# From which block on GpSimd's conversions for a block are split behind the last sum of x: block 6 or block 4

## Chip, core and metric

The kernel runs on one core of a Trainium2 chip. The metric is the device time of one execution in microseconds. Before the change three runs took 195.11, 195.18 and 197.03 us; the median, 195.18 us, is the time to be compared. One execution more was recorded by the hardware profiler; all views of the profile are of that one.

## What is computed

A linear recurrence over the sequence (retention, 4 batches, 8 heads, 768 steps, head dimension 64), whose output is the input of a two-layer block with the Mish activation (width 512, inner width 2048):

```python
for t in range(S):
    state = gamma[None, :, None, None] * state + np.einsum('bhd,bhe->bhde', k[:, :, t], v[:, :, t])
    y[:, :, t] = scale * np.einsum('bhd,bhde->bhe', q[:, :, t], state)
...
x = np.ascontiguousarray(attn_out.transpose(0, 2, 1, 3)).reshape(B * S, H * D)
h = x @ w_in
sp = np.where(h > 20.0, h, np.log1p(np.exp(np.minimum(h, 20.0))))
g = h * np.tanh(sp)
return (g @ w_out).astype(np.float32)
```

## The kernel before

**Chunks and blocks.** The sequence of each batch is cut into chunks of 128 rows, 6 a batch, 24 in all. Chunks are numbered 0 to 23. Block 0 holds chunks 0 to 3, and each of blocks 1 to 10 holds two: block 4 holds chunks 10 and 11, block 6 holds 14 and 15, block 7 holds 16 and 17. As a batch has 6 chunks, the work repeats every three blocks: blocks 4 and 7 do the same on TensorE, and so do blocks 5 and 8.

**One block, from block 4 on.** `mixed_in` (L844) makes h = x·w_in, partly by plain products (L875) and partly by a seven-product scheme for 2x2 halves (L855), which needs four sums of x, and adds its partial results on VectorE (L890); ScalarE applies Mish (L866). `seven` (L927) makes g·w_out by seven products (L949); ScalarE copies partial results (`snap`, L955), and VectorE adds them into the output tile `osb` (`done`, L964 and L962). Within `seven` lies the recurrence of later blocks: `retain` (L585) finishes the scores of the next block, and `ready` (L496) begins the block behind that, from the transposed q and k (`qkt`) and from v. So `seven` of block 4 needs the q, k and v of chunks 14 and 15.

**The sums of x.** `x_sums` (L838) makes the four sums, as fp16 differences in SBUF, on VectorE, one instruction each (L842). Two stand behind the fourth output addition of the block before, two at its end. They are the last thing that VectorE does in `seven`; behind them come the state (L513 to L528) and the mask (L548) of the block to come, and then the additions L890, for which TensorE waits.

**What GpSimd does.** It converts q, k and v of each chunk from fp32 to scaled fp16: q at L422, k at L425 (`casts_qk`), v at L432 (`casts_v`), one instruction each. `cast_behind(blk, i)` (L1274), called in `seven`, first copies one element of a sum of g (L1277), so that GpSimd starts behind that sum, and then converts the two chunks of block blk + 3: both q and k, then both v. Where blk + 1 >= `BACK` it converts only the q and k of the first chunk there. The rest is left to `second_of` (L1246), which the main loop calls ahead of the next block's `mixed_in`: it copies one element of the last sum of x (L1249), and then converts q and k of the second chunk and both v.

**SyncE's queue.** Every load (L162), every transpose of q and k by DMA (L437, `turn_by_dma`) and every store (L234, L1232) is issued by SyncE, in program order. Eight semaphores are used in turn, so a DMA is not issued until the one eight before it has landed. In `next_two` (L1234) both chunks are transposed and then two more are loaded; in `next_one` (L1241) one chunk is loaded and the first chunk is transposed, and the second transpose, the stores and another load follow in `second_of`. `osb` has 5 buffers (two a block), q has 4 load buffers, k and v 6 each.

**What the constants decide.** `ONE`, `MIX` and `BACK` are 3, 4 and 6. The main loop (L1317 to L1347) uses `BACK` in three places: whether `second_of(blk - 1)` is called ahead of block blk (blk >= BACK), whether `seven` of block blk calls `next_one` or `next_two` (blk + 1 >= BACK), and which branch `cast_behind` takes (blk + 1 >= BACK).

Of the kernel before, what the change touches and what calls it, by code (L numbers as in the profile page):

```python
# [16 lines left out]
def kernel(  # L17
# [101 lines left out]
    loaded, cast, qkts, ats, ams, states, mids, us, ys = {}, {}, {}, {}, {}, {}, {}, {}, {}  # L119
    xts, gts, wins, wouts, wtmps = {}, {}, {}, {}, {}  # L120
    gtiles, tmats, gsums = {}, [], []
    ONE, MIX, BACK = 3, 4, 6
    nload, ncast = [0], [0]
    stores, weight_left, wsums = [], [], []

# [1253 lines left out]
```

## Time and profile before

| | |
|---|---|
| median of three runs | 195.18 us |
| the profiled execution: its own time | 197.2 us |
| its span, from the first to the last instruction | 195.4 us |
| TensorE busy | 189.2 us, 97% |
| VectorE busy | 141.5 us, 72% |
| ScalarE busy | 104.1 us, 53% |
| GpSimd busy | 73.8 us, 38% |
| granted TensorE clock | 1.000 |

The profiled execution took 1.8 us more than its span, and 2.0 us more than the median of the runs. Times below are counted from the start of its span. Engines are PE (TensorE matmul), PEld (its weight load), DVE (VectorE), ACT (ScalarE), POOL (GpSimd) and SP (SyncE; SPq its DMA queue). An entry in brackets at the end of a row is the time that the engine sat idle before it, and what released it.

By TensorE's first matmul of `mixed_in` (L855) and of `seven` (first L949 behind it), block 4 runs from 92.78 to 108.33 us, block 5 to 123.27, block 6 to 137.48, block 7 to 151.53 and block 8 to 165.57.

### The profile page before, as it was taken

How to read it: one execution, taken by the hardware profiler on the slowest of the kernel's cores; microseconds unless marked ns; L12 is line 12 of the kernel's file. 1: busy time of each engine (PE TensorE's matmuls, PEld its weight loads, DVE VectorE, ACT ScalarE, POOL GpSimd, SP SyncE). 2: the span in 40 equal slices, each digit the busy share in tenths (PEclk: the TensorE clock that was granted, in tenths of full speed). 3: DMA queues.
4: the chain of work that ended last, by engine and by line, in shares of the span. 5: the costliest groups of instructions: out<-in, count | busy, mean ns of one | idle time of the engine just before them, and what ended most of it. 6: DMA issues, size and time to landing. Idle time of an engine off the chain costs nothing.

```text
span 195.4 us, 7191 instructions
## 1 busy us (share of the span) xinstructions
PE 189.2 (97%) x3124; PEld 161.8 (83%) x3124; DVE 141.5 (72%) x270; ACT 104.1 (53%) x194; POOL 73.8 (38%) x98
## 2 busy tenths in 40 slices
PE   7998999999999999999989999999999999999993
PEld 7756478888888888888968978998998998988993
DVE  0796559886686787987995995965885885875462
ACT  3375766263633633644574574484574664763850
POOL 5362000579209629904807605535625710000000
DMA  5999999999999999999799799979894250300202
GB/s 174 303 311 352 361 386 363 304 305 200 218 233 258 224 243 209 166 269 210 159 235 265 138 244 279 100 189 256 101 251 89 53 152 3 111 0 22 92 29 81
DMA packets 84303, 38.78 MB, mean 198 GB/s; under 512 B 57776, under 2 KB 78896, under 8 KB 84272
## 3 DMA queue, kind: packets, MB, share of 16 engines
q1 hardware_dynamic: 84128, 38.28, 81.8%
q8 instruction: 24, 0.39, 0.9%
q14 instruction: 7, 0.06, 0.1%
q10 hardware_dynamic: 144, 0.05, 0.1%
HBM read 27.31 MB, written 6.29 MB: 172 GB/s over the span
## 4 chain that ended last, share of the span: by engine, by line
PE 87%; DVE 6%; ACT 2%; DMA 2%; issue 1%; POOL 0%; POOLq 0%; DVEq 0%
PE o_ps L949 29%; PE h_ps L646 17%; PE h_ps L875 10%; PE h_ps L855 10%; PE o_ps L703 7%; PE at L451 4%; PE y_ps L559 3%; DMA out_dram<-osb 2%; PE t_ps L255 2%; DVE xt L842 1%; DVE hsum L890 1%; PE u_ps L487 1%; PE at L480 1%; ACT g L866 1%; PE y_ps L381 1%
## 5 line engine op out<-in xcount | busy, mean ns | idle before, releaser
L646 PE MATMUL h_ps<-xt,win 128*128 128x256 f16 (+1 forms) x272 | 34.3, 285 | 0.0
L949 PEld LDWEIGHTS <-gsum 128*128 128x128 f16 x320 | 30.3, 98 | 3.8
L646 PEld LDWEIGHTS <-win 128*128 128x128 f16 x272 | 26.4, 98 | 6.5
L655 ACT ACTIVATE g<-h_ps 128x512 f16<-128x512 f32 x38 | 22.7, 597 | 15.6 <-PE h_ps L646 15.6
L949 PE MATMUL o_ps<-tmat,gsum 128*128 128x256 f16 x240 | 29.8, 273 | 0.0
L875 PE MATMUL h_ps<-xt,win 128*128 128x256 f16 x224 | 29.0, 273 | 0.0
L949 PEld LDWEIGHTS <-g 128*128 128x128 f16 x248 | 23.3, 98 | 3.3 <-ACT g L866 0.6
L964 DVE TENSOR_TENSOR osb<-o_ps,snap 128x256 f32<-128x256 f32 (+1 forms) x33 | 13.7, 417 | 12.9 <-PE o_ps L949 7.6
L955 ACT COPY snap<-o_ps 128x256 f32<-128x256 f32 (+1 forms) x33 | 12.2, 370 | 20.1 <-PE o_ps L949 20.1
L875 PEld LDWEIGHTS <-win 128*128 128x128 f16 x224 | 20.8, 98 | 2.0
L866 ACT ACTIVATE g<-h_ps 128x512 f16<-128x512 f32 x35 | 19.9, 588 | 3.4 <-PE h_ps L875 3.4
L885 ACT COPY hsum<-h_ps 128x512 f32<-128x512 f32 x21 | 12.3, 585 | 14.9 <-PE h_ps L855 14.9
L425 POOL TENSOR_TENSOR qk<-kf,qvs 128x512 f16<-128x512 f32 x18 | 19.0, 1056 | 1.7 <-DMA kf<-in_k_dram 1.7
L422 POOL TENSOR_TENSOR qk<-qf,qvs 128x512 f16<-128x512 f32 x18 | 19.1, 1064 | 1.2 <-DMA qf<-in_q_dram 1.2
L949 PE MATMUL o_ps<-wout,g 128*128 128x256 f16 x160 | 19.4, 273 | 0.1
L432 POOL TENSOR_TENSOR v<-vf,qvs 128x512 f16<-128x512 f32 x18 | 19.1, 1076 | 0.4 <-DMA vf<-in_v_dram 0.3
L1277 POOL COPY summed<-gsum 128x1 f16<-128x1 f16 x7 | 3.0, 422 | 42.9 <-DVE gsum L815 32.1
L890 DVE TENSOR_TENSOR hsum<-h_ps,hsum 128x512 f32<-128x512 f32 x21 | 14.1, 688 | 6.1 <-PE h_ps L855 4.3
L855 PE MATMUL h_ps<-xt,wsum 128*128 128x128 f16 x224 | 15.9, 219 | 0.0
L608 ACT CAST xt<-y_ps 128x512 f16<-128x512 f32 x15 | 10.2, 735 | 10.4 <-PE y_ps L559 10.4
L866 ACT ACTIVATE g<-hsum 128x512 f16<-128x512 f32 x21 | 13.2, 630 | 4.0 <-DVE hsum L890 4.0
L855 PEld LDWEIGHTS <-wsum 128*128 128x128 f16 x224 | 14.0, 98 | 0.4
(112 smaller groups left out, 303.2 us busy)
## 6 DMA issues: line engine op xcount, KB each, us to landing
kf<-in_k_dram SPq DMA_DIRECT2D x24, 256.0 KB, 5.2
vf<-in_v_dram SPq DMA_DIRECT2D x24, 256.0 KB, 5.4
out_dram<-osb SPq DMA_DIRECT2D x22, 256.0 KB, 3.7
qf<-in_q_dram SPq DMA_DIRECT2D x20, 256.0 KB, 5.4
wi<-in_moe_w_in_dram SPq DMA_DIRECT2D x6, 512.0 KB, 8.8
wt<-in_moe_w_out_dram SPq DMA_DIRECT2D x2, 1024.0 KB, 10.3
wt<-in_moe_w_out_dram SPq DMA_DIRECT2D x4, 512.0 KB, 7.6
qfirst<-in_q_dram SPq DMA_DIRECT2D x2, 512.0 KB, 4.6
```

Source lines behind the costliest of these rows:

```text
L422: nc.gpsimd.tensor_tensor(in_place(q16.rearrange("p (w x) d -> p w x d", x=2)), by_head(qf), scale_by_head(qs_two[:, heads]), op=ALU.mult)
L425: nc.gpsimd.tensor_tensor(k16.rearrange("p (y w) d -> p w y d", y=2), kf.rearrange("p (w y) d -> p w y d", y=2), boosts.rearrange("p (w y) ...
L432: nc.gpsimd.tensor_tensor(cast[g][2], loaded.pop(g)[2], vs[g % 2].unsqueeze(2).broadcast_to((P, H, D)), op=ALU.mult)
L646: nc.tensor.matmul(h_ps[:, j, cols], wins[s][f // 2][:, bp, f % 2 * P:(f % 2 + 1) * P], xts[blk][:, bp, cols], start=(bp == 0 and at == 0) ...
L655: nc.scalar.activation(gt, h_ps, AF.Mish, scale=inv_boost3)
L703: nc.tensor.matmul(banks[ij][:, t], x(f)[:, t * P:(t + 1) * P], w(f), start=ij in open_banks, stop=f == fs[-1], skip_group_check=True)
L855: nc.tensor.matmul(o_ps[:, f], w(f // 2, k)[:, f % 2 * P:(f % 2 + 1) * P], x[:, k], start=begin and f == 0 and k == 0, stop=k == 1, skip_g ...
L866: nc.scalar.activation(to, src, AF.Mish, scale=inv_boost3)
L875: nc.tensor.matmul(h_ps[:, f], wins[w][h // 2][:, k, h % 2 * P:(h % 2 + 1) * P], xts[blk][:, k, :2 * C], start=k == 0, stop=k == NBP - 1)
L890: nc.vector.tensor_tensor(m, x, y, op=ALU.add)
L949: nc.tensor.matmul(o_ps[:, cols], x(f), w(f)[:, cols], start=first and z == 0, stop=z == n - 1, skip_group_check=True)
L964: nc.vector.tensor_tensor(dst, o_ps[:, cols], plus, op=ALU.add)
```

## The change

One constant goes from 6 to 4. The program's comparisons with it then hold two blocks sooner:

```diff
-    ONE, MIX, BACK = 3, 4, 6
+    ONE, MIX, BACK = 3, 4, 4
```

The code that it steers:

```python
def second_of(blk):
    g = first[blk] + 6
    if g < NCK:
        nc.gpsimd.tensor_copy(summed, xts[blk + 1][:, 3, TB - 1:])
        casts_qk(g + 1)
        turn_by_dma(g + 1)
        casts_v(g)
        casts_v(g + 1)
    store_due(NFB)
    load_to(g + 4)
...
def next_two(g):
    for n in range(2):
        turn_next(g + n)
    if g == first[ONE] + 6:
        store(2)
    load_to(g + 4)

def next_one(g):
    load_to(g + 3)
    if g < NCK:
        turn_by_dma(g)
...
        elif blk + 1 >= BACK:          # in cast_behind
            cast_to(g - 2)
            casts_qk(g - 2)
            ncast[0] = g
```

In GpSimd's order this moves, for chunks 14 to 17, the second chunk's q and k and both v behind one more one-element copy each (two instructions are added, none is taken out). In SyncE's order it moves these DMAs; their number stays:

- before: transposes of 14 and 15; two stores (block 2's); loads of 16 and 17; two stores (block 3's); transposes of 16 and 17; loads of 18 and 19; two stores (block 4's); load of 20
- after: load of 16; transposes of 14 and 15; four stores (blocks 2's and 3's); loads of 17 and 18; transposes of 16 and 17; two stores (block 4's); loads of 19 and 20

TensorE's, VectorE's and ScalarE's instructions and their order stay as they are.

## The prediction, made before the changed kernel was run

> **What bounds the kernel now.** I read the table of engines first, then the chain of waits, then the stretches block by block, and then the rows of single engines around the two longest blocks.
>
> ```profile
> PE 189.2 (97%) x3124; PEld 161.8 (83%) x3124; DVE 141.5 (72%) x270; ACT 104.1 (53%) x194; POOL 73.8 (38%) x98
> ```
>
> TensorE sets the time: what does not fill one of its gaps is worth nothing. The chain that ended last shows where it has gaps: from 97.03 to 115.03 us it leaves TensorE and runs through VectorE, ScalarE and one store, in blocks 4 and 5 only; in blocks 6 to 9 it is TensorE throughout. So I asked for the busy times by stage, `mixed_in` of blocks 4, 5, 7 and 8 and `seven` of 4 (columns: stretch, its length, busy time and instructions of each engine, granted clock, DMA):
>
> ```profile
> 92.78:100.68 7.90, 7.13 (x90) 6.32 (x88) 7.79 (x14) 4.65 (x9) 4.03 (x4) 1.00 0.85 199
> 100.68:108.33 7.65, 7.62 (x178) 6.49 (x176) 5.03 (x12) 3.78 (x8) 4.29 (x5) 1.00 0.95 231
> 108.33:115.62 7.29, 6.89 (x90) 6.29 (x88) 7.19 (x14) 4.64 (x9) 2.37 (x3) 1.00 0.96 193
> ...
> 137.48:144.17 6.69, 6.69 (x90) 6.25 (x88) 5.62 (x12) 4.94 (x9) 4.19 (x5) 1.00 0.81 139
> ...
> 151.53:158.22 6.69, 6.69 (x91) 6.25 (x89) 5.63 (x12) 4.95 (x9) 4.18 (x5) 1.00 0.49 119
> ```
>
> `mixed_in` takes 7.90 us in block 4 and 7.29 in block 5 (VectorE busy almost all of it), against 6.69 in blocks 7 and 8, which do the same work at the same clock. TensorE's rows name the wait: block 4's last seven-product matmuls (L855) wait for VectorE's addition L890, and VectorE reaches that late because the four sums of x ahead of it are slow. VectorE's time in L842 around the end of blocks 3, 4, 5 and 6:
>
> ```profile
> 100.13 0.61 PE L855 MATMUL h_ps<-xt,win 128*128 128x128 f16 x8 [0.76 <-DVE hsum L890]
> ```
>
> ```profile
> 91.60:95.95 4.35, 3.61 (x4) 1.00 0.70 130
> 107.15:110.90 3.75, 3.00 (x4) 1.00 0.79 130
> 122.10:124.30 2.20, 1.07 (x4) 1.00 1.53 162
> 136.30:138.55 2.25, 1.07 (x4) 1.00 1.69 199
> ```
>
> Four equal instructions: 3.61 and 3.00 us in the first two places, 1.07 in the others. What differs is GpSimd. Its rows at the first place, and VectorE's:
>
> ```profile
> 91.57 1.04 POOL L425 TENSOR_TENSOR qk<-kf,qvs 128x512 f16<-128x512 f32 x1
> 92.57 1.09 POOL L422 TENSOR_TENSOR qk<-qf,qvs 128x512 f16<-128x512 f32 x1
> 93.62 1.09 POOL L425 TENSOR_TENSOR qk<-kf,qvs 128x512 f16<-128x512 f32 x1
> 94.67 2.14 POOL L432 TENSOR_TENSOR v<-vf,qvs 128x512 f16<-128x512 f32 x2
> ```
>
> ```profile
> 91.67 2.13 DVE L842 TENSOR_TENSOR xt<-xt 128x256 f16<-128x256 f16 x2
> 93.73 0.41 DVE L964 TENSOR_TENSOR osb<-o_ps,snap 128x256 f32<-128x256 f32 x1
> 94.06 0.41 DVE L962 COPY osb<-o_ps 128x256 f32<-128x256 f32 x1
> 94.39 1.51 DVE L842 TENSOR_TENSOR xt<-xt 128x256 f16<-128x256 f16 x2
> ```
>
> GpSimd changes instruction at 92.57, 93.62, 94.67 and (half of 2.14 on) 95.7. The first sum ends at 92.75, the second at 93.8, the third at 94.86, the fourth at 95.9: each just behind the next such change, however early it began. The additions between them, which read PSUM, keep their 0.41 us. So a sum of x waits until the GpSimd instruction under way is over. The Trainium skill, "SBUF — State Buffer", section "SBUF: two separate sides", gives a reason: VectorE instructions with two SBUF inputs and GpSimd's share a port pair, an exclusive lock held for the whole instruction. By that rule the trace agrees, with 1.02 to 1.13 us for a sum under GpSimd against the shortest row of 0.279.
>
> **Part 1, conversions moved out of the sums of x.** At the end of block 3, GpSimd's q and k of chunk 14 stay (90.57 to 92.6); chunk 15's q and k and both v, four instructions of 1.04 to 1.09 us, move behind the sums. The first sum still waits for 92.6 and ends at 92.75; the second then takes 0.28 (93.0). The additions L964 and L962 follow at their present spacing of 0.33 (TensorE's operands are there: block 6 does these 1.17 and 1.07 us after its matmul starts, here 92.2 and 93.0), then two sums at 0.27: the end is 94.2 instead of 95.9. VectorE is 1.7 us earlier. From TensorE's start of the block that is 1.42 us, against 1.03 in block 7 (138.51 less 137.48): 0.4 late still. Block 7's second L890 sits idle 0.36 and its third 0.40, waiting for ScalarE and TensorE; that cover takes up the 0.4, so block 4 runs as block 7. It gains 7.90 - 6.69 = 1.21 in `mixed_in`. Its `seven` starts with 16 plain matmuls that need Mish of the late sums: from the first L949 to the 17th is 1.94 us in blocks 4 and 5, and 1.75 in block 7 and 1.74 in block 8; 0.19 goes too. Block 4: 1.40.
>
> At the end of block 4, chunk 16's q and k are done 2.04 us after GpSimd's release (106.55 of the present count), and the sums begin at 107.22: 0.67 later, the same gap as block 5 has now (121.49 and 122.16), where four sums take 1.07. All of it goes: 7.29 - 6.69 = 0.60, and 0.20 in `seven`. Block 5: 0.80.
>
> Sum: 2.20 us. The rest of `seven` is 0.1 us longer in each of blocks 4 and 5 than in 7 and 8 (5.71 and 5.61), spread over the small matmuls of the recurrence; no wait stands beside it. I count 0, with 0.2 as its upper bound.
>
> **Part 2, two one-element copies on GpSimd.** 0.19 us each where they have been seen behind a sum of x (0.52 behind a sum of g). Behind them queue four conversions, 4.1 us, and whoever needs them: in block 4 they run from 94.2 to 98.6. VectorE's next instructions with two SBUF inputs are L528 and the sums of g; in block 7 L528 starts 6.56 us into the block, so here at 99.3, 0.7 clear. `seven` needs the v from its L487 at 104.80, which the gain puts at 103.4. Price: 0; if the cover goes, up to one conversion of 1.04 us per instruction caught.
>
> **Part 3, SyncE's queue.** The load of 16 goes ahead of the transpose of 14, three issues of 0.5 to 1.1 us from 90.14: the transpose, ready at 92.64, slips by 0 to 1 us and is needed at 103.7. The transpose of 15 waits for its k until 96.5, not 94.73; rows of the same step have issues of 1.23 to 2.66 us and landings 3.1 to 5.4 us behind the start: 99.6 to 101.9, needed at 103.7. Behind it queue block 2's two stores, which stand at 96.06 now, then block 3's. They are issued from 97.8 to 98.4 on, and landing takes 1.6 to 4.8 us: the first is out by 103.2 at the latest. `osb` has five buffers, so block 4's second tile reuses block 2's first. It is written by the L964 ahead of the sums of x, now at 106.84, then at 105.4: 2.2 us clear. (The profile puts 1.59 us of idle before that L964 to a store that landed at 106.85. But block 7's same L964 also starts 5.87 us after its first L949, for TensorE; here it is 6.16, of which 0.19 is the slow start. I take the store for a coincidence, worth at most 0.1.) Chunk 17 is loaded behind these stores, from about 100.3; 4.4 to 6.0 us to landing gives 107 for q and k, which GpSimd wants at 108 and 109. The chain of eight semaphores adds at most a wait for the first store in front of 18's loads, which nobody wants before 117. From block 6 on the order is as it is. Price: 0, for those margins.
>
> **The profiled execution and the median.** Taken from the profiled execution: 197.2 - 2.2 = 195.0. Its 2.0 us over the median have no place that I can name; both waits come out of program order and fixed durations, so the whole 2.2 is taken from the median too: 195.18 - 2.20 = 193.0 us. One per cent, 1.95 us or 193.23, is about what a measurement of this kernel can tell from no change.
>
> **Rivals.**
> - The 0.4 us by which block 4's sums stay late does reach TensorE (the third L890 moves by it, or Mish does): gain 1.75, time 193.4. For it: the chunk-14 conversion does overlap the first sum. Against it: the idle entries of 0.36 and 0.40. Chance 0.13.
> - Moved conversions catch later VectorE instructions: if GpSimd starts 0.7 us or more later than I put it, L528 and then the sums of g wait, one conversion each. One or two at 1.04 us in block 4 take half the gain: 194.0, at most 194.3. Against it: block 7 has these rows 1.2 us clear. The page's rule named above says the same of any instruction with two SBUF inputs, and gives no other price. Chance 0.08.
> - It does nothing: the sums are slow for another reason, the DMA traffic or the state of the chip, and stay at 3 us: 195.2. Against it: DMA share is 0.70 and 0.79 there, and 1.53 and 1.69 where they are fast. Chance 0.07.
> - Slower: block 2's stores, now behind the transpose of 15, hold block 4's L964, and with it the sums of x, 1 us for 1 us. It takes from 105.4 on; the gain is eaten at 107.6, and 1% is lost at 109.5, 11 to 12 us after issue, against 4.8 at most in the rows. Four stores and six loads in a row speak for some delay. If one lands at 109.6, the time is 197.2. Chance 0.07.
>
> **How the numbers follow.** The forecast itself has 0.65: a gain of 1.9 to 2.5 us, 192.7 to 193.3. The range takes in the first two rivals and the spread of a median, a few tenths: 192.5 to 194.4. That leaves out the last two rivals, 0.14, and a little of the tails. Faster by over 1%: nearly nine tenths of the forecast's own, 0.57. Slower: 0.07. Within: 0.36.
>
> **What would show it.** In the changed profile: L842 in block 3's end 1.9 to 2.0 us for four (one slow), in block 4's end 1.07; no idle of TensorE before block 4's and 5's last L855; both `mixed_in` at 6.7 us; L964 ahead of the sums waiting for TensorE, not for a store; GpSimd's copy L1249 at about 94.2, and its conversions over before L528. The forecast is wrong if a sum is slow with GpSimd idle, or if a store or a transpose stands as releaser in block 4 or 5.

## The result, and the profile after

| | before | after |
|---|---|---|
| median, 22 runs each | 195.94 us | 194.93 us |
| lowest to highest | 194.87 to 197.22 us | 194.80 to 196.50 us |
| ratio of the times, 95% interval | | 0.9946 [0.9923, 0.9968] |
| profiled execution, its span | 197.2, 195.4 us | 195.02, 193.2 us |

The change gains 1.0 us in the median, half a per cent, and not 2.2. Yet the two profiled executions differ by just the 2.2 that were forecast (195.4 and 193.2). Both are true: the runs before spread over 2.3 us, of which the profiled one was at the upper end, and 18 of the 22 runs after lie between 194.80 and 195.02. The lowest runs of the two kernels are within 0.1 us of each other.

The stretches of the changed kernel, `mixed_in` and `seven` of blocks 4 and 5 in turn (columns: stretch, length, busy time and instructions of PE, PEld, DVE, ACT, POOL, clock, DMA share, GB/s):

```profile
92.77:99.46 6.69, 6.69 (x91) 6.26 (x89) 6.12 (x14) 5.05 (x9) 4.18 (x5) 1.00 1.29 189
99.46:107.00 7.54, 7.54 (x180) 6.68 (x178) 4.89 (x13) 3.57 (x8) 2.51 (x3) 1.00 1.08 290
107.00:113.69 6.69, 6.69 (x91) 6.26 (x89) 5.63 (x12) 4.97 (x9) 4.18 (x5) 1.00 1.15 159
113.69:121.14 7.45, 7.45 (x179) 6.57 (x177) 4.94 (x13) 3.56 (x8) 2.51 (x3) 1.00 1.15 269
```

TensorE is busy through all of them; 7.90, 7.65, 7.29 and 7.65 us have become 6.69, 7.54, 6.69 and 7.45, together 2.12 less. VectorE's and GpSimd's rows at the end of block 3:

```profile
91.66 1.41 DVE L842 TENSOR_TENSOR xt<-xt 128x256 f16<-128x256 f16 x2
92.99 0.42 DVE L964 TENSOR_TENSOR osb<-o_ps,snap 128x256 f32<-128x256 f32 x1
93.32 0.41 DVE L962 COPY osb<-o_ps 128x256 f32<-128x256 f32 x1
93.65 0.48 DVE L842 TENSOR_TENSOR xt<-xt 128x256 f16<-128x256 f16 x2
```

```profile
91.56 1.04 POOL L425 TENSOR_TENSOR qk<-kf,qvs 128x512 f16<-128x512 f32 x1
94.27 0.19 POOL L1249 COPY summed<-xt 128x1 f16<-128x1 f16 x1 [1.67 <-DVE xt L842]
```

Only the first sum still waits, for the conversion of chunk 14's k; the four take 1.89 us instead of 3.61. And the output addition ahead of the sums of block 5, the one that block 2's stores might have held, waits for TensorE:

```profile
105.51 0.42 DVE L964 TENSOR_TENSOR osb<-o_ps,snap 128x256 f32<-128x256 f32 x1 [1.68 <-PE o_ps L949]
```

So the question is not where 1.1 us of the gain went in the changed kernel, but why most executions of the kernel before, in this measurement, did not have 2.2 us to lose.

### The profile page after: what moved, and what is told of

Read it like the earlier page. It is cut to its first block, busy times and chain, and to the rows that moved or that the text cites. A ratio compares the mean times of both kernels' runs of the same rounds, so it can differ in the third digit from the quotient of the medians.

```text
span 193.2 us, 7199 instructions
## 1 busy us (share of the span) xinstructions
PE 188.3 (97%) x3124; PEld 162.2 (84%) x3124; DVE 138.3 (72%) x270; ACT 104.4 (54%) x194; POOL 74.0 (38%) x100
## 4 chain that ended last, share of the span: by engine, by line
PE 96%; ACT 1%; issue 1%; POOL 0%; DVE 0%; POOLq 0%
PE o_ps L949 32%; PE h_ps L646 17%; PE h_ps L875 13%; PE h_ps L855 12%; PE o_ps L703 7%; PE at L451 4%; PE y_ps L559 3%; PE t_ps L255 2%; PE u_ps L487 1%; PE at L480 1%; PE y_ps L381 1%; PE h_ps L628 1%; PE at L335 1%; PE u_ps L353 1%; PE y_ps L391 0%
## 5 line engine op out<-in xcount | busy, mean ns | idle before, releaser
L949 PEld LDWEIGHTS <-gsum 128*128 128x128 f16 x320 | 30.3, 98 | 3.9
L949 PE MATMUL o_ps<-tmat,gsum 128*128 128x256 f16 x240 | 29.7, 273 | 0.0
L949 PEld LDWEIGHTS <-g 128*128 128x128 f16 x248 | 23.4, 98 | 2.6
L949 PE MATMUL o_ps<-wout,g 128*128 128x256 f16 x160 | 19.1, 273 | 0.0
```

The costliest lines, as they stand in the source:

```text
L949: nc.tensor.matmul(o_ps[:, cols], x(f), w(f)[:, cols], start=first and z == 0, stop=z == n - 1, skip_group_check=True)
```

## Experiments

In all of them the kernel before was run again beside the others, in three sessions on three chips; its medians there were 197.12, 197.07 and 197.16 us (194.96 to 198.06, and two runs of 198.70 and 199.56). The ratios with their intervals compare a version with the kernel before in the same session; they are not the quotients of the medians, and where the runs of a kernel spread over 2 us the two can differ by half a per cent. The edits are shown against the changed kernel, except where the text says that the kernel before is edited. Theory A: what the lock costs (the time that VectorE's sums wait for GpSimd's conversions) varies by itself. Theory B: it costs a constant 2.2 us, and SyncE's new order gives 1.1 back. Theory C came up after the first four runs.

**The kernel before, again.** No edit.

> The kernel before, unchanged, for another profiled execution. Its 22 runs spread from 194.87 to 197.22 us, and the profiled one took 197.2. Theory A (the lock costs a different amount in each execution): where the execution takes less than 197, TensorE's wait in mixed_in of blocks 4 and 5 (7.90 and 7.29 us against 6.69) is shorter by about the same amount, and the rows of L842 at the ends of blocks 3 and 4 (3.61 and 3.00 us for four) are shorter too. Theory B (the lock costs 2.2 us in every execution, and the spread comes from elsewhere, so the change gives back about 1.1 us through SyncE's new order): 7.90 and 7.29 stay within 0.1 us whatever the total, and the difference lies in another stretch.

It took 197.58 us, with 7.90 and 7.28 us in `mixed_in` of blocks 4 and 5. An execution of the upper end again; it does not tell the theories apart.

**SyncE's order alone.** GpSimd's order stays that of the kernel before:

```diff
-    ONE, MIX, BACK = 3, 4, 4
+    ONE, MIX, BACK, SPLIT = 3, 4, 4, 6
...
-            nc.gpsimd.tensor_copy(summed, xts[blk + 1][:, 3, TB - 1:])
-            casts_qk(g + 1)
+            split = blk + 1 >= SPLIT
+            if split:
+                nc.gpsimd.tensor_copy(summed, xts[blk + 1][:, 3, TB - 1:])
+                casts_qk(g + 1)
             turn_by_dma(g + 1)
-            casts_v(g)
-            casts_v(g + 1)
+            if split:
+                casts_v(g)
+                casts_v(g + 1)
...
-            elif blk + 1 >= BACK:
+            elif blk + 1 >= SPLIT:
```

> SyncE's order as in the changed kernel, GpSimd's as before (both chunks converted at once, no copies added). Theory A: SyncE's order costs and gains nothing; ratio to before 0.997 to 1.003, four L842 at the ends of blocks 3 and 4 as slow as before (3 to 3.7 us in an execution of 197 us). Theory B: the order alone costs about 1.1 us, ratio about 1.006.

197.16 us, ratio 1.0004 [0.9972, 1.0036]; four sums took 3.61 and 3.00 us, as before. Whatever the order costs or gains is under 0.4%, and the 1.006 of theory B lies outside the interval. The half of theory B that is about SyncE's order falls.

**Block 5 alone.** `BACK = 5`.

> The constant at 5: block 4 as before, block 5 as in the changed kernel (GpSimd split behind the sums at the end of block 4, SyncE's order from there). Theory A: of a gain of 1.06 us (median) the share of block 5, 0.80 of 2.20, is kept: ratio about 0.998, highest runs near 196.4 instead of 197.2, mixed_in of block 5 at 6.7 us and of block 4 at 6.7 to 7.9. Theory B: the split in block 5 is worth 0.8 and the order costs some of it: ratio 0.998 to 1.000, but block 4 at 7.90 in every profile.

196.35 us (195.01 to 197.11), ratio 0.9962 [0.9934, 0.9989], which is a larger gain than either theory had named, though 0.998 lies inside the interval. Its profiled execution took 195.91 us and held the clue. Block 5 took 6.69 us in `mixed_in`; block 4, not split, took 7.37 and not 7.90, and GpSimd's rows there show why:

```profile
91.65 1.04 POOL L425 TENSOR_TENSOR qk<-kf,qvs 128x512 f16<-128x512 f32 x1
93.21 1.04 POOL L422 TENSOR_TENSOR qk<-qf,qvs 128x512 f16<-128x512 f32 x1 [0.52 <-DMA qf<-in_q_dram]
```

GpSimd stood idle for 0.52 us, waiting for chunk 15's q. The second sum of x ran in that gap: its pair took 1.41 us, as in the changed kernel, against 2.13. So block 4 is not at 7.90 in every profile, as theory B had it. From this came theory C: the loads of chunks 15 and 17 land at another time in each execution, and where they land late, the conversions keep out of the way of the sums by themselves.

**Two more blocks unsplit.** `BACK = 8`.

> The constant at 8: the conversions of blocks 6 and 7 too lie across the sums of x (ends of blocks 5 and 6), as in blocks 4 and 5 before. Theory A: each of them adds what block 5 adds in an execution, 0 to 0.8 us: median 0.4 to 1.0 us slower than before, ratio 1.002 to 1.005, highest runs near 198.8, and four L842 at the ends of blocks 5 and 6 longer than 1.07 us. Theory B: 0.8 us each in every execution: 1.6 us slower, ratio 1.008, lowest run not under 196.4.

198.75 us (197.12 to 199.61), ratio 1.0083 [1.0048, 1.0118]: 1.6 us slower. The blocks that took 6.69 now take what block 5 took before (`mixed_in` of blocks 6 and 7):

```profile
123.28:130.57 7.29, 6.89 (x91) 6.30 (x89) 6.61 (x12) 4.62 (x9) 2.36 (x3) 1.00 0.95 179
138.28:145.51 7.23, 6.89 (x90) 6.29 (x88) 7.13 (x14) 4.62 (x9) 2.30 (x3) 1.00 0.87 185
```

The sums of x at the ends of blocks 5 and 6, which took 1.07 us for four, now take about 3:

```profile
122.17 1.52 DVE L842 TENSOR_TENSOR xt<-xt 128x256 f16<-128x256 f16 x2
124.28 1.51 DVE L842 TENSOR_TENSOR xt<-xt 128x256 f16<-128x256 f16 x2
...
137.18 1.46 DVE L842 TENSOR_TENSOR xt<-xt 128x256 f16<-128x256 f16 x2
139.22 1.51 DVE L842 TENSOR_TENSOR xt<-xt 128x256 f16<-128x256 f16 x2
```

So the stall was made in two more blocks, at 0.8 us a block. The size was theory B's, not the 0.4 to 1.0 of theory A; it was the full price here, and in this profile GpSimd waited for no load in any of the four blocks.

**The changed kernel again.** No edit.

> The changed kernel again, beside new runs of the kernel before. Theory C (the lock costs up to 2.2 us, but only in an execution in which the loads of chunks 15 and 17 land in time for GpSimd to be converting while VectorE makes the sums; where they land late, GpSimd stands idle and the sums are free): the changed kernel stays at 194.8 to 195.0 us in nearly all runs, and the ratio follows the kernel before: about 0.995 where its median is 195.9, about 0.989 where it is 197.1. Theory B (a constant 2.2 less a constant cost of the new order): the difference of the medians is 1.0 to 1.1 us wherever it is measured.

195.09 us in six runs, before 197.07: ratio 0.9917 [0.9885, 0.9950], a difference of 1.98. The changed kernel takes within 0.2 us the time of the first measurement; the kernel before is 1.1 us off it. Theory C had said 0.989 for such a median, which lies inside the interval. A constant 1.0 to 1.1 us would be 0.9944 to 0.9949; by the medians it is too small, but the interval just takes it in, so this run alone does not rule it out.

**Chunk 15's q and k four DMAs later**, block 4 unsplit (`BACK = 5`), in `turn_four`:

```diff
-        load_to(g + 6)
+        load_to(g + 5)
+        room(g + 5)
+        room(g + 6)
+        for c, n in ((g + 5, 2), (g + 6, 0), (g + 6, 1), (g + 6, 2), (g + 5, 0), (g + 5, 1)):
+            load_one(c, n, nc.sync)
+        nload[0] = g + 7
```

> Constant at 5 (block 5 split, block 4 not), and chunk 15's q and k are loaded behind chunk 16's three loads instead of ahead of them, about four DMAs later. No instruction of GpSimd or VectorE is changed. Theory C: GpSimd waits for q of chunk 15 until about 96 us, the sums at the end of block 3 run free (about 1.9 us for four, as in the changed kernel, or 1.5), and block 4's mixed_in takes 6.7 us: median 194.9 to 195.2, ratio as the changed kernel's. Theory A (the cost of the lock varies by itself, not through the loads): as with the constant at 5 alone, 195.0 to 197.1, median 196.35.

196.57 us (195.74 to 198.05), ratio 0.9995 [0.9963, 1.0027]: not the time that theory C gave. The profiled execution, of 195.74 us, was the fastest of the twelve. In it chunk 15's q, issued at 91.03, landed 5.8 us later, GpSimd stood idle until 97.07, and block 4's `mixed_in` did take 6.69 us, but its `seven` took 8.24 instead of 7.54:

```profile
98.07 1.04 POOL L425 TENSOR_TENSOR qk<-kf,qvs 128x512 f16<-128x512 f32 x1
99.07 2.22 POOL L432 TENSOR_TENSOR v<-vf,qvs 128x512 f16<-128x512 f32 x2
```

```profile
99.34 1.06 DVE L528 TENSOR_TENSOR sth<-suh,gch 128x256 f16<-128x256 f32 x1
100.32 1.26 DVE L810 TENSOR_TENSOR gsum<-g 128x512 f16<-128x512 f16 x1
101.61 0.42 DVE L811 TENSOR_TENSOR gsum<-gsum,g 128x512 f16<-128x512 f16 x1
```

The conversions, too late now, caught L528 and the first sum of g (0.42 us each without them), and TensorE waited for the sums of g. That is the second rival of the prediction, at the place it named, for 0.7 us, though in another kernel than the one it was named for. The median lies 0.8 us above this execution, and no profile shows where the slower ones lost it. The room is narrow: the sums end at 94.1 and L528 starts at 99.3, so four conversions of 1.04 us must start between 94.1 and 95.1 to touch neither.

**Chunk 15's q and k two DMAs later.** As above, with the order v15, q16, q15, k15, k16, v16.

> Constant at 5, chunk 15's q and k loaded two DMAs later (behind v of 15 and q of 16) instead of four. Block 4's conversions stay unsplit. Theory C: q of chunk 15 lands near 94.5, behind the sums of x, and the conversions are over near 99, ahead of the sums of g: in the executions in which it falls so, block 4 takes 6.7 and about 7.5 us and the run 194.9 to 195.2, without a split. Runs in which it lands sooner or later by a microsecond lose up to 1.4. Median 195.2 to 196.0, lowest at 195.0. Theory A: median 196.35 as with the constant at 5 alone.

195.15 us (194.94 to 197.15), ratio 0.9951 [0.9915, 0.9988]. Eight of twelve runs lie under 195.3: the changed kernel's time is reached with GpSimd's order for block 4 left alone. The profiled execution was one of the others (196.71), and yet its block 4 was fast. GpSimd's q waited until 97.89, 3.5 us into the block; `mixed_in` took 6.69 us and `seven` 7.61. The first sum of g took 1.27 us, as in the run above, but here that cost TensorE less than 0.2 us. What made this execution slow lies ahead of block 4, which began at 94.38 instead of 92.78; 0.95 us of that is a wait for a transposed tile in block 3, whose transpose stands ahead of the moved loads in SyncE's order:

```profile
84.78 0.38 PE L480 MATMUL at<-qkt 64*64 64x64 f16 x24 [0.95 <-DMA qkt<-qk]
```

```profile
97.89 1.04 POOL L422 TENSOR_TENSOR qk<-qf,qvs 128x512 f16<-128x512 f32 x1 [3.68 <-DMA qf<-in_q_dram]
```

**Chunk 15's q and k sooner**, `BACK = 5`, in `turn_four`:

```diff
-        store(2)
-        load_to(g + 6)
+        store(1)
+        for c in (g + 4, g + 5):
+            room(c)
+        for n in range(3):
+            for c in (g + 4, g + 5):
+                load_one(c, n, nc.sync)
+        nload[0] = g + 6
+        store(1)
```

> Constant at 5, and chunk 15's q and k are loaded sooner: of block 1's two stores one goes behind the loads, and the loads are in the order q14, q15, k14, k15, v14, v15. Theory C: chunk 15 is there in every execution, so block 4's mixed_in takes 7.90 us in every one and the runs gather at 196.3 (194.9 plus 1.40), hardly one under 196. Theory A: the spread stays as with the constant at 5 alone, 195.0 to 197.1, a third of the runs under 195.7.

196.50 us, and all twelve runs between 196.37 and 196.80; ratio 0.9984 [0.9960, 1.0007]. The spread of 2.1 us that `BACK = 5` alone had in the first session has shrunk to 0.43, and 196.4 to 196.5 is the changed kernel's 195.0 plus the 1.40 of block 4. Its profile has 7.91 us in block 4's `mixed_in`, and GpSimd's rows for chunk 15 show no wait:

```profile
93.01:100.92 7.91, 7.14 (x91) 6.33 (x89) 7.79 (x14) 4.66 (x9) 4.04 (x4) 1.00 0.84 206
```

```profile
92.80 1.09 POOL L422 TENSOR_TENSOR qk<-qf,qvs 128x512 f16<-128x512 f32 x1
93.86 1.08 POOL L425 TENSOR_TENSOR qk<-kf,qvs 128x512 f16<-128x512 f32 x1
```

**Both pairs sooner, the kernel before otherwise.** The same in `turn_four`, and in `next_two` for chunks 16 and 17.

> The kernel before, constant at 6, with the loads of both pairs 14/15 and 16/17 in the order q, q, k, k, v, v and one of two stores behind them, so that the second chunk's q and k land sooner. Theory C: GpSimd never waits, both places cost their full 1.40 and 0.80 us in every execution: median 2.0 to 2.3 us over the changed kernel's 195.0, that is 197.0 to 197.4, spread of most runs under 0.6 us, none under 196.5; so equal to the upper half of the runs before, and slower than their median by 0 to 1 us. Theory A: the spread of the kernel before (more than 2 us) stays.

197.48 us (197.18 to 199.06), ratio 1.0058 [1.0024, 1.0092]; 7.91 and 7.29 us in blocks 4 and 5 of the profiled execution. None of the twelve runs is under 197.18, and 15 of the 29 runs of the kernel before beside them are: the fast executions are gone. Sooner data, slower kernel. Nine runs lie within 0.5 us of the lowest; three took 197.91, 198.00 and 199.06, and no profile shows why.

**The changed kernel with 14 and 15 sooner.** The same edit of `turn_four` at `BACK = 4`.

> The changed kernel with the loads of 14 and 15 in the order q, q, k, k, v, v and one of block 1's stores behind them. Theory C: with the split the early loads cost nothing, and a load that lands late can no longer push the conversions into the sums of g: 194.8 to 195.1 in nearly all runs, median as the changed kernel's (ratio to it 0.999 to 1.001), fewer runs over 195.5. Rival: the store moved behind the loads holds block 3's output tiles, and it is slower by some tenths.

195.18 us (194.89 to 197.40), ratio to the kernel before 0.9939 [0.9904, 0.9974]: about the changed kernel's time, not better. Six of the twelve runs lie in the 194.8 to 195.1 that were expected of nearly all; five took 195.28 to 195.43, and one 197.40. In the profiled execution, of 195.28 us, blocks 4 and 5 took 6.69, 7.45, 6.69 and 7.46 us, so with the split the earlier landing cost nothing there; 0.3 us were lost ahead of block 4. Of the versions tried none beats the changed kernel.

**The kernel before, a third and a fourth time.**

> The kernel before, for a third profiled execution. Theory C: what it takes beyond 194.9 us is TensorE's wait in blocks 4 and 5, and where that is short of 2.2 us, GpSimd shows a wait for a load of chunk 15 or 17 (DMA qf or kf) ahead of its second q or k.

197.98 us; 7.92 and 7.29 us in blocks 4 and 5, and no wait of GpSimd. Another 0.8 us lay ahead of block 4, so, against the expectation, not all that an execution takes beyond 194.9 us is this stall.

> The kernel before, for a fourth profiled execution; the three so far took 197.2 to 198.0 us. Theory C: at 197 us or more no wait for a load ahead of the second chunk's q and k and 7.9 and 7.3 us in blocks 4 and 5; at less, a wait and a shorter block.

This one took 195.01 us, as little as the changed kernel. The stretches of `mixed_in` of blocks 4 and 5, and GpSimd's rows for the second chunk's q and k in the two places:

```profile
92.82:99.51 6.69, 6.69 (x90) 6.25 (x88) 6.21 (x14) 4.96 (x9) 4.22 (x4) 1.00 0.97 102
...
106.97:113.65 6.68, 6.68 (x90) 6.25 (x88) 6.02 (x12) 4.99 (x9) 4.09 (x4) 1.00 1.25 197
```

```profile
92.86 1.17 POOL L422 TENSOR_TENSOR qk<-qf,qvs 128x512 f16<-128x512 f32 x1 [0.20 <-DMA qf<-in_q_dram]
95.15 1.04 POOL L425 TENSOR_TENSOR qk<-kf,qvs 128x512 f16<-128x512 f32 x1 [1.11 <-DMA kf<-in_k_dram]
...
107.14 1.04 POOL L422 TENSOR_TENSOR qk<-qf,qvs 128x512 f16<-128x512 f32 x1 [1.51 <-PE o_ps L949]
109.08 1.04 POOL L425 TENSOR_TENSOR qk<-kf,qvs 128x512 f16<-128x512 f32 x1 [0.90 <-DMA kf<-in_k_dram]
```

The unchanged kernel, with no stall at all: GpSimd waits 1.31 us at the first place and 2.41 at the second, and the sums of x slip through (2.05 and 1.60 us for four). The third row's releaser is given as TensorE, but chunk 17's q, issued at 102.02 here and at 99.92 in the first profiled execution, took 5.0 us to land and so was there at 107.0, just ahead of the conversion: this wait was for the load too.

## Why the prediction was wrong

- **What bounds the kernel, and Part 1: right.** The first profiled execution lost 1.21 and 0.60 us in `mixed_in` and 0.20 twice at the head of `seven`; the changed one has all of that back (the 17th L949 of `seven` comes 1.74 us after the first in both blocks). The sums at the end of block 3 end at 94.13, against 94.2 forecast, and the 0.4 us by which they stay late is covered. The rest of block 4's `seven` took 0.09 more, so the sum is 2.12; in the second profile of the changed kernel (195.19 us) the four stretches are 6.69, 7.46, 6.68 and 7.46 us, and the sum is 2.20. That GpSimd's conversions make the sums slow is shown by `BACK = 8`, where putting conversions across the sums made them slow in two more places, and by L528 and L810 in the late run, which took 1.06 and 1.26 us beside conversions and 0.42 without. A sum of x took 0.46 to 1.13 us beside conversions in the first profile, by how much of the conversion under way was left (the prediction's 1.02 to 1.13 leaves out the shorter ones), and 0.28 without. This is what the Trainium skill, "SBUF — State Buffer", section "SBUF: two separate sides", says of instructions with two SBUF inputs, and the numbers agree.
- **Part 2: right.** The conversions end at 98.45, L528 starts at 99.33 (forecast 98.6 and 99.3).
- **Part 3: right in its sum.** The ratio of the order alone is 1.0004. In detail the transpose of 14 slipped by 1.76 us (94.40), not by 0 to 1, and it did no harm; the first store left at 98.31.
- **The profiled execution and the median: this step failed.** I wrote that both waits "come out of program order and fixed durations, so the whole 2.2 is taken from the median too". GpSimd's second conversions do not start by program order alone; where q and k land later than that, they start when these have landed. The rows were there: q of chunk 15 was issued at 86.14 and landed 5.9 us later, at 92.0, for a conversion at 92.57; k at 88.75 and 4.4, 93.15, for one at 93.62. A margin of half a microsecond; I worked out such margins for transposes, stores and loads of the changed kernel and for none of the kernel before. In all five profiles in which block 4's `mixed_in` took 7.9 us with its loads left in their order, q and k of chunk 15 had landed, 0.5 to 1.0 us ahead of their conversions; in the two in which it took less, q or k was what GpSimd waited for. And the times said it: the profiled execution without the stall is 197.2 - 2.2 = 195.0, and two of the three runs shown, 195.11 and 195.18, are that already, so they had no 2.2 us to lose. I noted the 2.0 us between the profiled execution and the median, could not name their place, and carried the gain over whole. Their place was this stall: the fourth profile of the kernel before, of 195.01 us, is without it. What the change gains in the median is 1.0 us beside a median of 195.94 and 1.98 us beside one of 197.07.
- **The rivals.** None took the share of the missing 1.1 us: what was missing was a rival in which the loss is there in some executions only. The conversions that catch later instructions, given 0.08, did not come in the changed kernel; they came in the late run, where GpSimd's first one began at 97.07 and not at 94.41.

What stays open: why the kernel before has a median of 195.94 us in the first measurement and of 197.1 in the three later sessions. By the account above its loads were in time more often there, but no run shows that, nor whether it would be the chip or chance. Not all of the spread is this stall either: in the profiles block 4 begins between 92.8 and 94.4 us. Three of the 28 runs of the changed kernel took 195.87, 196.27 and 196.50 us, and none of them was profiled.

## What to carry to other kernels

Ask of a stall in one profile whether it is there in every execution: if the profiled time is above the median by about the stall, as 197.2 was above 195.18, it may well not be, and then only the share that the median has can be gained. A stall between two engines that depends on when a load lands is found by the margin between landing and use in the slow version, and settled by moving that load some places either way. Work that must not run beside other work should wait for it, as the changed kernel's one-element copy makes it do; a late load that happens to keep them apart is not an order.

## What was not expected of the hardware

The same 256 KB load of chunk 15's k, issued at 88.75 and at 89.26 us in two executions of one program, took 4.4 us to land in the one and 5.8 us in the other, so that GpSimd had it at 93.15 and at 95.1. Conversions of 1.04 us queued back to back on GpSimd did not keep VectorE out: in the first profiled execution each of the eight sums of x at the two places ran at the next change of GpSimd's instruction, which cost GpSimd about 0.05 us an instruction (1.09 instead of 1.04).
